# A linear-attention and MLP block: M built from whole 80-column windows inside tile 0's product, Q's weights permuted on chip, and six more short zero matmuls at the start

## The chip, the cores and the metric

The kernel runs on one core of one Trainium2 chip. The metric is the device time in microseconds of one execution. The kernel before took 210.43 us, the median of 9 runs (209.28 to 211.49).

## The reference

Everything is in bf16, with S = 2048 tokens, D = 640, 32 heads of 20 dimensions, and F = 1536. Cut to what matters:

```python
xn = layernorm(x)
# A: linear attention
q, k, v = split(xn @ wqkv)                     # 32 heads of 20
phi = lambda t: where(t > 0, t + 1, exp(t)) + 1e-6
pq, pk = phi(q), phi(k)
kv  = einsum("bhsd,bhse->bhde", pk, v)         # per head 20 x 20
z   = sum over s of pk
num = einsum("bhqd,bhde->bhqe", pq, kv)
den = einsum("bhqd,bhd->bhq", pq, z) + 1e-6
A = (num / den) @ wo
# B: MLP
B = gelu(xn @ w1 + b1) @ w2 + b2
out = x + A + B
```

## The kernel before

A small planner (`Planner.ins`) records every instruction by hand in the order of its engine's queue, works out which semaphores it has to wait for from the resources it reads and writes, and leaves out waits that the engine already knows of and TensorE's waits for itself. Each engine then runs its own list in order. Nothing is reordered later: the order in the source is the order on each queue.

The tokens are 16 tiles of 128, in 4 chunks of 512. D is 5 blocks of 128 and F is 12. The eight banks of PSUM are handed out in a ring (`take`).

1. **Start (L255 to L425).** SP loads x tile by tile and W1 in four pieces. `filler(9)` runs nine 512-column matmuls on zeros on TensorE. VectorE and GpSimd work out tile 0's norm, TensorE transposes tile 0 (`transp2`, L313), ScalarE and VectorE copy it to `xnT` (L321, L322), a tiny transpose (L303) turns b1, one more filler follows, and then the units of the MLP's first product begin (`h_unit`, L381: five matmuls and a gelu on ScalarE, L385). Tiles 1 and 2 are transposed by TensorE among the units ("T1" and "T2" in `plan`), all later tiles by DMA (`xnT_dma`, L245) after VectorE's norm (L354). Units of tiles 0 to 3 take one tile each, then two pairs of tiles, then two groups of four.
2. **K (L475 to L484).** 160 matmuls (L480) and `phi`: exp on ScalarE (L468), two steps on VectorE (L469, L471).
3. **G (L489 to L497).** G = xn^T phi(K), 160 matmuls (L492) into `GTb`, while VectorE sums phi(K) over the tiles into `zsum` in fp32 (L501, L504) and splits the sum into a high and a low bf16 part `zhl` (L506, L507).
4. **Q (L525 to L533).** For each chunk and each j of 5, five 512-column matmuls (L529) and `phi`. The 128 rows of block j are the columns j, j+5, j+10, ... of Q's weights, so each head has four rows in each block, and the weights are loaded with a step of 5. After chunk 0 come `z_step` (z per row, L512, and the masked `ZB`, L518) and `kvt_step` (L538): V's weights times G, masked by VectorE to the heads' blocks (L542), into the zeroed `KVT`.
5. **M and the denominator (L546 to L575).** M = blockdiag(kv) Wo in Q's row order (`m_step`): for each j and each half of the columns, two windows of rows by four groups of 32 columns of the array, 80 matmuls (L554), copied to `Msb` by ScalarE (L563) or VectorE (L560). Then `den_all`: 20 matmuls (L569), + 1e-6 (L573) and the reciprocal (L575).
6. **Spread and scale.** `spread` copies the reciprocals, 32 heads per chunk, by four DMAs of 32 KB per chunk to the 128 rows of Q's layout (`rsp`); chunk 0's are issued by ScalarE, the others by SP. `scale_pq` multiplies a chunk of phi(Q) by it in one VectorE step (L579). `x_again` (SP) loads x once more.
7. **Output (L612 to L662).** `out_mm` accumulates, for each tile, 12 products of the gelu with W2 and 5 of phi(Q) with M, in two halves of 320 columns (L618). The W2 part of tiles 0 to 3 is done first, then their phi(Q) part, then tiles 4 to 15 in one go; VectorE adds x + b2 (L594, L629) and SP stores. The last tile goes in pieces of 320, 192 and 128 columns.

Of the kernel before, what the change touches and what calls it, by code (L numbers as in the profile page):

```python
# [5 lines left out]
ALU = AluOpType  # L6
ACT = mybir.ActivationFunctionType
P = 128
# [104 lines left out]
def bass_parallel_sum__linear_attn_block__dense_activation_gelu__prompt_kernel(  # L113
# [13 lines left out]
    assert DH == 4 * DT and NC == 4 and P == 4 * H and DT * F >= 2 * (DT + 1) * D  # L127
# [4 lines left out]

    e0 = [DH * ((P * t) // DH) for t in range(DT)]
    e1 = [DH * (-((-(P * (t + 1))) // DH)) for t in range(DT)]
    Wd = [e1[t] - e0[t] for t in range(DT)]

    with contextlib.ExitStack() as es:
# [15 lines left out]
        KVT = W1f[:, DT * D:2 * DT * D].rearrange("p (k d) -> p k d", k=DT)  # L153
        Wqkv = sb("Wqkv", [P, DT, 3 * D], BF16)
        W2 = sb("W2", [P, JT, D], BF16)
        Wo = sb("Wo", [P, DT, D], BF16)
# [9 lines left out]
        hmask = sb("hmask", [P, H], BF16)  # L166
        maskKV = [sb(f"maskKV{t}", [P, Wd[t]], BF16) for t in range(DT)]
# [11 lines left out]
        rsp = sb("rsp", [P, NC, CW], BF16)  # L179
# [31 lines left out]
        r_Wq, r_Wv, r_W2, r_Wo = R_("Wq"), R_("Wv"), R_("W2"), R_("Wo")  # L211
# [12 lines left out]
        r_KVT = R_("KVT")  # L224
        r_M = [R_("M%d" % j) for j in range(DT)]
        r_zsum, r_zhl, r_z, r_ZB = R_("zsum"), R_("zhl"), R_("z"), R_("ZB")
        r_den, r_rden = R_("den"), R_("rden")
        r_rsp = [[R_("rsp%d_%d" % (c, r)) for r in range(4)] for c in range(NC)]
# [59 lines left out]
        for t in range(DT):  # L288
            band(maskKV[t][:], r_masks, P * t - e0[t], Wd[t] // DH, DH)
        band(hmask[:], r_hmask, 0, H, 4)  # L290
# [5 lines left out]
        def filler(n):  # L296
            b = take(1)
            Pl.ins(pe, [lambda e: e.matmul(bank(b), warm[:, 0:P], warm[:], start=True, stop=True)  # L298
                        for _ in range(n)], reads=[r_warm], writes=[B_[b]])
# [93 lines left out]
        filler(9)  # L393
        ln_half(0, 0)
# [60 lines left out]
        dma("sync", Wo[:], A_wo.rearrange("(k p) n -> p k n", p=P), [r_Wo])  # L455
# [31 lines left out]
        Pl.ins(g, lambda e: e.memset(KVT.bitcast(FP32), 0.0), writes=[r_KVT] + r_W1)  # L487
# [11 lines left out]
        def z_sums():  # L499
            a, c = tord[0], tord[1]  # L500
            Pl.ins(v, lambda e: e.tensor_tensor(out=zsum, in0=PK[:, a, :], in1=PK[:, c, :], op=ALU.add),  # L501
                   reads=[r_PK[a], r_PK[c]], writes=[r_zsum])
            for t in tord[2:]:
                Pl.ins(v, lambda e, t=t: e.tensor_tensor(out=zsum, in0=zsum, in1=PK[:, t, :], op=ALU.add),  # L504
                       reads=[r_PK[t], r_zsum], writes=[r_zsum])
            Pl.ins(v, lambda e: e.tensor_copy(zhl[:, 0, :], zsum), reads=[r_zsum], writes=[r_zhl])  # L506
            Pl.ins(v, lambda e: e.tensor_tensor(out=zhl[:, 1, :], in0=zsum, in1=zhl[:, 0, :], op=ALU.subtract),  # L507
                   reads=[r_zsum, r_zhl], writes=[r_zhl])

        def z_step():  # L510
            b = take(1)
            Pl.ins(pe, [(lambda e, j=j, i=i: e.matmul(bank(b, j, j + 1), zhl[:, i, j:D:DT], onesm[:, 0:1],  # L512
                                                      start=(i == 0), stop=(i == 1)))
                        for j in range(DT) for i in range(2)],
                   reads=[r_zhl, r_ones], writes=[B_[b]])
            Pl.ins(v, lambda e: e.tensor_copy(z_sb[:], bank(b, 0, DT)), reads=[B_[b]], writes=[r_z])
            for j in range(DT):
                Pl.ins(v, lambda e, j=j: e.tensor_scalar(ZB[:, j, :], hmask[:], z_sb[:, j:j + 1], None, ALU.mult),  # L518
                       reads=[r_z, r_hmask], writes=[r_ZB])
# [5 lines left out]
        def q_chunk(c):  # L525
            cc = slice(c * CW, (c + 1) * CW)
            for j in range(DT):
                b = take(1)
                Pl.ins(pe, [(lambda e, k=k, j=j, b=b: e.matmul(  # L529
                    bank(b), Wqkv[:, k, j:D:DT], xnT[:, k, cc],  # L530
                    start=(k == 0), stop=(k == DT - 1))) for k in range(DT)],
                    reads=[r_Wq] + sum(r_xnT[c * CH:(c + 1) * CH], []), writes=[B_[b]])
                phi(bank(b), b, 1, PQ[:, j, cc], r_PQ[c][j], [])  # L533

        def kvt_step():
            for t in range(DT):
                b = take(1)
                Pl.ins(pe, [(lambda e, k=k, b=b, t=t: e.matmul(  # L538
                    bank(b, 0, Wd[t]), Wqkv[:, k, 2 * D + t * P:2 * D + (t + 1) * P],
                    GTb[:, k, e0[t]:e1[t]], start=(k == 0), stop=(k == DT - 1))) for k in range(DT)],  # L540
                    reads=[r_Wv] + r_GT, writes=[B_[b]])
                Pl.ins(v, lambda e, b=b, t=t: e.tensor_tensor(  # L542
                    out=KVT[:, t, e0[t]:e1[t]], in0=bank(b, 0, Wd[t]), in1=maskKV[t][:], op=ALU.mult),
                    reads=[B_[b], r_masks], writes=[r_KVT])

        def m_step():  # L546
            for j in range(DT):
                b = (0, 2, 4, 0, 2)[j]
                fns = []
                for h in range(2):  # L550
                    for i in range(2):
                        for q in range(4):
                            c0 = j + 32 * DT * q
                            fns.append(lambda e, t=q + i, q=q, i=i, h=h, b=b, c0=c0: e.matmul(  # L554
                                bank(b + h, 0, HW)[32 * q:32 * q + 32, :],
                                KVT[:, t, c0:c0 + 31 * DT + 1:DT], Wo[:, t, h * HW:(h + 1) * HW],
                                start=(i == 0), stop=(i == 1)))
                Pl.ins(pe, fns, reads=[r_KVT, r_Wo], writes=B_[b:b + 2])
                if j in (2, 4):
                    Pl.ins(v, lambda e, b=b, j=j: e.tensor_copy(halves(Msb[:, j, :]), pair(b)),  # L560
                           reads=B_[b:b + 2], writes=[r_M[j], r_zsum, r_zhl])
                else:
                    Pl.ins(s_, lambda e, b=b, j=j: e.activation(halves(Msb[:, j, :]), pair(b), ACT.Copy),  # L563
                           reads=B_[b:b + 2], writes=[r_M[j], r_zsum, r_zhl])

        def den_all():
            b = 6
            for j in range(DT):
                Pl.ins(pe, [(lambda e, j=j, c=c: e.matmul(  # L569
                    bank(b)[H * c:H * c + H, :], ZB[:, j, :], PQ[:, j, c * CW:(c + 1) * CW],  # L570
                    start=(j == 0), stop=(j == DT - 1))) for c in range(NC)],
                    reads=[r_ZB] + [r_PQ[c][j] for c in range(NC)], writes=[B_[b]])
            Pl.ins(v, lambda e: e.tensor_single_scalar(den_sb[:], bank(b), 1e-6, ALU.add),  # L573
                   reads=[B_[b]], writes=[r_den])
            Pl.ins(v, lambda e: e.reciprocal(rden[:], den_sb[:]), reads=[r_den], writes=[r_rden])  # L575

        def scale_pq(c):
            cc = slice(c * CW, (c + 1) * CW)
            Pl.ins(v, lambda e: e.tensor_tensor(  # L579
                out=PQ[:, :, cc], in0=PQ[:, :, cc],  # L580
                in1=rsp[:, c:c + 1, :].broadcast_to((P, DT, CW)), op=ALU.mult),
                reads=r_rsp[c] + r_PQ[c], writes=r_PQ[c])

        def spread(c):
            for r in range(4):
                dma(s_ if c == 0 else "sync", rsp[r:P:4, c, :], rden[H * c:H * c + H, :], [r_rsp[c][r]],
                    reads=[r_rden])
# [14 lines left out]
        ring[0] = 3  # L602
# [3 lines left out]
        m_step()  # L606
        den_all()
        for c in range(NC):
            spread(c)
        scale_pq(0)  # L610

        def out_mm(t, lo, hi, b, w0, w1):  # L612
            tok = slice(t * P, (t + 1) * P)
            seq = [(HG[:, jb, tok], W2[:, jb, :], [r_HG[t][jb], r_W2]) for jb in range(JT)]
            seq += [(PQ[:, j, tok], Msb[:, j, :], [r_PQ[t // CH][j], r_M[j]]) for j in range(DT)]
            n = len(seq)
            for i in range(lo, hi):
                Pl.ins(pe, [(lambda e, i=i, x=x, bb=bb: e.matmul(  # L618
                    bank(bb, 0, x[1] - x[0]), seq[i][0], seq[i][1][:, x[0]:x[1]],
                    start=(i == 0), stop=(i == n - 1))) for x, bb in zip(w0, w1)],  # L620
                    reads=seq[i][2], writes=[B_[bb] for bb in w1], mark=(i in (JT - 1, n - 1)))
# [12 lines left out]
        ahead = [4, 0, 2, 6]  # L634
        for t, b in enumerate(ahead):
            out_mm(t, 0, JT, b, HALF, [b, b + 1])
# [6 lines left out]
        ring[0] = 4  # L643
# [7 lines left out]
        t = NT - 1  # L651
        xb(t)
# [49 lines left out]
```

## Time and profile before

| | |
|---|---|
| median of 9 runs | 210.43 us (209.28 to 211.49) |
| the nine runs | 209.28, 209.30, 209.71, 209.78, 210.43, 210.69, 210.98, 211.40, 211.49 |
| profiled execution, its own time | 210.98 us |
| its span, first to last instruction | 209.3 us |
| TensorE busy | 205.1 us (98%) |
| VectorE / ScalarE / GpSimd busy | 108.5 / 74.4 / 20.1 us |
| chain that ended last: TensorE | 96% of the span |

The profile is one execution. Times in it are microseconds from the span's start unless marked ns. An engine that is not the bottleneck loses nothing by being idle. Matmuls are pipelined, so the length of one in the profile is more than the distance to the next one; distances between starts, or counts in a window, tell the pace. Where a line of the profile names an idle time, it also names what ended it; "issue" is time in which the engine waited for nothing that the profile shows.

### The profile page before, as it was taken

Reading aid. Unit: us, or ns where it says so; the run is one execution under the profiler, and the core shown is the slowest. Engines: PE = TensorE matmul, PEld = TensorE weight load, DVE = VectorE, ACT = ScalarE, POOL = GpSimd, SP = SyncE. Lnnn points to the kernel's source line nnn. Section 1 sums busy time; section 2 is a strip of 40 time slices with the busy share of each in tenths; the row PEclk is TensorE's granted clock in tenths of the full one; section 3 lists DMA queues with packets and bytes.
Section 4 is the critical chain, followed back from the end, with each engine's and each line's share of the span. In section 5 each row is a group of like instructions: output and inputs, shape, how many; then the busy total and the mean of one; then the engine's idle time right before and its main releaser. Section 6 shows DMA issues by size and latency. Waiting matters only on the chain.

```text
span 209.3 us, 3967 instructions
## 1 busy us (share of the span) xinstructions
PE 205.1 (98%) x1622; PEld 142.5 (68%) x1622; DVE 108.5 (52%) x213; ACT 74.4 (36%) x146; POOL 20.1 (10%) x57
## 2 busy tenths in 40 slices
PE   7999999999999999999999999999999999999995
PEld 2799888444457777777757556677777777777775
DVE  4588864000005888999048898733753422523322
ACT  2499888666667544211153556100000000000000
POOL 2144436700011000000000000000000000000000
DMA  5975995899300000000000001952110110000002
GB/s 166 351 242 103 134 169 105 267 307 376 115 0 0 0 3 0 3 0 0 0 3 0 0 2 21 357 170 61 63 66 31 53 45 31 31 34 31 31 31 66
DMA packets 23371, 18.16 MB, mean 87 GB/s; under 512 B 9912, under 2 KB 23352, under 8 KB 23352
## 3 DMA queue, kind: packets, MB, share of 16 engines
q1 hardware_dynamic: 23136, 17.77, 29.4%
q8 instruction: 13, 0.21, 0.4%
q10 hardware_dynamic: 216, 0.13, 0.3%
q14 instruction: 6, 0.05, 0.1%
HBM read 12.62 MB, written 2.62 MB: 73 GB/s over the span
## 4 chain that ended last, share of the span: by engine, by line
PE 96%; DVE 1%; DMA 1%; issue 0%
PE ps L618 35%; PE ps L381 26%; PE ps L492 10%; PE ps L480 10%; PE ps L529 10%; PE ps L554 1%; DMA xPK<-in_A_x_dram 1%; DVE stats L326 1%; PE ps L538 1%; PE ps L313 1%; PE ps L569 1%; PE ps L298 0%; PE ps L512 0%; DVE W L659 0%; DVE xn_tm L354 0%
## 5 line engine op out<-in xcount | busy, mean ns | idle before, releaser
L618 PE MATMUL ps<-W,HG 128*128 128x320 bf16 (+2 forms) x396 | 54.6, 295 | 0.0
L381 PE MATMUL ps<-xnT,W 128*128 128x128 bf16 (+2 forms) x480 | 54.3, 277 | 0.1
L381 PEld LDWEIGHTS ps<-xnT,W 128*128 128x128 bf16 x480 | 38.2, 101 | 15.8 <-issue 0.5
L618 PEld LDWEIGHTS ps<-W,HG 128*128 128x128 bf16 x396 | 38.1, 98 | 14.6 <-issue 0.4
L385 ACT ACTIVATE HG<-ps,b1c 128x128 bf16<-128x128 f32 (+2 forms) x96 | 41.8, 474 | 13.4 <-PE ps L381 11.7
L629 DVE TENSOR_TENSOR W<-ps,xnT 128x640 bf16<-128x640 f32 x15 | 12.4, 824 | 36.9 <-PE ps L618 36.6
L468 ACT ACTIVATE ek<-ps 128x512 bf16<-128x512 f32 (+1 forms) x36 | 23.2, 645 | 20.7 <-PE ps L529 11.0
L469 DVE TENSOR_SCALAR ek<-ek 128x512 bf16<-128x512 bf16 (+1 forms) x36 | 10.9, 303 | 37.8 <-ACT ek L468 36.6
L618 PE MATMUL ps<-Msb,PQ 128*128 128x320 bf16 (+2 forms) x165 | 24.2, 295 | 0.0
L529 PE MATMUL ps<-xnT,Wqkv 128*128 128x512 bf16 x100 | 21.9, 379 | 0.0
L492 PE MATMUL ps<-xPK,xn_tm 128*128 128x320 bf16 x160 | 21.9, 299 | 0.0
L480 PE MATMUL ps<-Wqkv,xnT 128*128 128x320 bf16 x160 | 21.9, 299 | 0.0
L618 PEld LDWEIGHTS ps<-Msb,PQ 128*128 128x128 bf16 x165 | 15.9, 98 | 5.9
L480 PEld LDWEIGHTS ps<-Wqkv,xnT 128*128 128x128 bf16 x160 | 15.7, 98 | 6.2
L492 PEld LDWEIGHTS ps<-xPK,xn_tm 128*128 128x128 bf16 x160 | 15.7, 98 | 6.1
L529 PEld LDWEIGHTS ps<-xnT,Wqkv 128*128 128x128 bf16 x100 | 11.7, 118 | 9.5
L326 DVE BATCH_NORM_STATS2 stats<-xPK 128x6 f32<-128x320 bf16 x32 | 15.1, 472 | 4.2 <-DMA xPK<-in_A_x_dram 3.6
L471 DVE SCALAR_TENSOR_TENSOR PQ<-ps,ek 128x512 bf16<-128x512 f32 x20 | 13.8, 691 | 2.1
L471 DVE SCALAR_TENSOR_TENSOR xPK<-ps,ek 128x640 bf16<-128x640 f32 x16 | 13.2, 824 | 1.7
L504 DVE TENSOR_TENSOR Msb<-Msb,xPK 128x640 f32<-128x640 f32 x14 | 11.6, 826 | 0.5
L496 ACT ACTIVATE W<-ps 128x640 bf16<-128x640 f32 x5 | 3.5, 704 | 18.2 <-PE ps L492 18.2
L354 DVE TENSOR_SCALAR xn_tm<-xPK,aggr,rstd 128x640 bf16<-128x640 bf16 (+2 forms) x17 | 7.3, 433 | 2.5 <-POOL rstd L342 1.3
(57 smaller groups left out, 77.9 us busy)
## 6 DMA issues: line engine op xcount, KB each, us to landing
xnT<-in_A_x_dram SPq DMA_DIRECT2D x4, 640.0 KB, 6.1
Wqkv<-in_A_wqkv_dram SPq DMA_DIRECT2D x3, 800.0 KB, 6.5
out_dram<-W SPq DMA_DIRECT2D x15, 160.0 KB, 1.8
W<-in_B_w_dram SPq DMA_DIRECT2D x4, 480.0 KB, 6.0
W<-in_B_w_dram SPq DMA_DIRECT2D x1, 1920.0 KB, 16.0
xPK<-in_A_x_dram SPq DMA_DIRECT2D x2, 640.0 KB, 6.3
Wo<-in_A_wo_dram SPq DMA_DIRECT2D x1, 800.0 KB, 10.6
xPK<-in_A_x_dram SPq DMA_DIRECT2D x4, 160.0 KB, 3.9
```

The lines of the kernel that those rows point to most:

```text
L326: Pl.ins(v, lambda e: e.bn_stats(stats[:, s, 6 * h:6 * h + 6], x_in[:, t, h * HW:(h + 1) * HW]), reads=r_x[t], writes=[r_stats[s]])
L381: Pl.ins(pe, [(lambda e, k=k: e.matmul(bank(b, 0, w), W1[:, k, jb * P:(jb + 1) * P], xnT[:, k, tok], start=(k == 0), stop=(k == DT - 1))) ...
L385: Pl.ins(s_, lambda e: e.activation(HG[:, jb, tok], bank(b, 0, w), ACT.Gelu_apprx_tanh, bias=b1c[:, jb:jb + 1]), reads=[B_[b], r_b1c], wri ...
L468: Pl.ins(s_, lambda e: e.activation(e2, src, ACT.Exp), reads=br, writes=[r_ek[s]])
L469: Pl.ins(v, lambda e: e.tensor_scalar(et, et, 1.0, 1e-6, ALU.min, ALU.add), reads=[r_ek[s]], writes=[r_ek[s]])
L471: Pl.ins(v, lambda e: e.scalar_tensor_tensor(out=d2, in0=src, scalar=0.0, in1=e2, op0=ALU.max, op1=ALU.add), reads=br + [r_ek[s]], writes= ...
L480: fns.append(lambda e, k=k, h=h, b=b, t=t: e.matmul(bank(b + h, 0, HW), xnT[:, k, t * P:(t + 1) * P], Wqkv[:, k, D + h * HW:D + (h + 1) * ...
L492: Pl.ins(pe, [(lambda e, t=t, h=h, b=b, f=f, i=i: e.matmul(bank(b + h, 0, HW), xn_tm[:, t, f * P:(f + 1) * P], PK[:, t, h * HW:(h + 1) * H ...
L504: Pl.ins(v, lambda e, t=t: e.tensor_tensor(out=zsum, in0=zsum, in1=PK[:, t, :], op=ALU.add), reads=[r_PK[t], r_zsum], writes=[r_zsum])
L529: Pl.ins(pe, [(lambda e, k=k, j=j, b=b: e.matmul(bank(b), Wqkv[:, k, j:D:DT], xnT[:, k, cc], start=(k == 0), stop=(k == DT - 1))) for k in ...
L618: Pl.ins(pe, [(lambda e, i=i, x=x, bb=bb: e.matmul(bank(bb, 0, x[1] - x[0]), seq[i][0], seq[i][1][:, x[0]:x[1]], start=(i == 0), stop=(i = ...
L629: Pl.ins(v, lambda e: e.tensor_tensor(out=halves(out_sb[:, s, :]), in0=pair(b), in1=halves(x_res[:, t, :]), op=ALU.add), reads=B_[b:b + 2] ...
```

## The change

- At the start, `filler` takes a width, and six 128-column zero matmuls follow the nine of 512 columns.
- The row order of Q's blocks is new. Blocks 0 and 1 hold dimensions 0 to 7 and 8 to 15 of heads 0 to 15, blocks 2 and 3 those of heads 16 to 31, and block 4 dimensions 16 to 19 of all 32 heads. GpSimd copies Q's weights in this order, 25 copies of 128 columns, over K's weights, which are no longer needed by then. Q's matmuls load them without a step; they wait for all 25 copies (`r_WqP`). `zhl` is written in the same order, in ten smaller VectorE steps.
- KV is built in 8 windows of 4 heads (80 columns), each over the 128 rows from `E0[w]`: 40 matmuls into two banks and three masking steps on VectorE. Wo is loaded as 8 overlapping windows of the same rows by 8 DMAs. Four GpSimd copies make from it `KVP`: the 32 columns of each window and block, side by side; for block 4, two windows share 32 columns and the other 16 are zero.
- M then takes, for each half of the columns, four matmuls per block (one window for each group of 32 columns) and eight for block 4: 48 instead of 80, in groups that each signal on their own; each half is copied by itself, the first by ScalarE and the second by VectorE.
- The order after Q: half the columns of tile 0's W2 product, the denominator's matmuls, M in the order 0, 1, 4, 2, 3 (den + 1e-6 on VectorE after the copies of block 1), the reciprocal, all spreads, the scaling of chunk 0, the other half of tile 0's W2 product into the bank that held the denominator, and then tiles 1 to 3.
- The spread is three DMAs of 128 KB per chunk, whose source repeats each head's row for 8 or 4 rows; all twelve are issued by ScalarE. `rsp` lies in the memory of `xn_tm`. A chunk is scaled in three VectorE steps.

The diff, cut to its core:

```diff
-        def filler(n):
+        def filler(n, w=512):
             b = take(1)
-            Pl.ins(pe, [lambda e: e.matmul(bank(b), warm[:, 0:P], warm[:], start=True, stop=True)
+            Pl.ins(pe, [lambda e: e.matmul(bank(b, 0, w), warm[:, 0:P], warm[:, 0:w], start=True, stop=True)
                         for _ in range(n)], reads=[r_warm], writes=[B_[b]])
...
         filler(9)
+        filler(6, P)
...
-        dma("sync", Wo[:], A_wo.rearrange("(k p) n -> p k n", p=P), [r_Wo])
+        for w in range(NW):
+            dma("sync", Wo[:, w, :], A_wo[E0[w]:E0[w] + P, :], [r_Wo[w]])
...
+        Pl.ins(g, lambda e: e.memset(KVP[2], 0.0), writes=[r_KVP[2]] + r_W1)
+        for k in range(DT):
+            for i in range(DT):
+                Pl.ins(g, lambda e, k=k, i=i: e.tensor_copy(plain(Wqkv[:, k, D:2 * D], i), parts(Wqkv[:, k, 0:D], i)),
+                       reads=[r_Wq], writes=[r_Wk, r_WqP])
...
-                    bank(b), Wqkv[:, k, j:D:DT], xnT[:, k, cc],
+                    bank(b), Wqkv[:, k, D + j * P:D + (j + 1) * P], xnT[:, k, cc],
...
+            for i in range(2):
+                Pl.ins(g, lambda e, i=i: e.tensor_copy(
+                    KVP[i].rearrange("p w (h t) -> p w h t", t=TA), kt[:, :, :, TA * i:TA * i + TA]),
+                    reads=r_KVT, writes=[r_KVP[i]] + r_W1)
...
+        def m_step(js, bs, after):
+            for n, (j, b) in enumerate(zip(js, bs)):
+                for h in range(2):
+                    fns, reads = [], []
+                    for a in range(2 if j == DT - 1 else 1):
                         for q in range(4):
...
+                    Pl.ins(pe, fns, reads=reads, writes=[B_[b + h]])
+                    m_copy(j, b, h)
+                if n == 1:
+                    after()
...
+            for r, (h, n) in enumerate(((0, HH), (HH, HH), (0, H))):
+                src = rdv[H * c + h:H * c + h + n].broadcast_to((n, P // n, CW))
+                dma(s_, rsp[:, c, r, :], src, [r_rsp[c][r]] + (sum(r_xn, []) if c + r == 0 else []),
                     reads=[r_rden])
...
-        m_step()
-        den_all()
-        for c in range(NC):
-            spread(c)
-        scale_pq(0)
+        b0 = take(2)
+        ahead = [(b0 + 2 * i) % 8 for i in range(4)]
...
-        ahead = [4, 0, 2, 6]
-        for t, b in enumerate(ahead):
+        out_mm(0, 0, JT, b0, HALF[:1], [b0])
+        den_mm(b0 + 1)
+        m_step([0, 1, DT - 1, 2, 3], ahead[1:] + ahead[1:3], lambda: den_eps(b0 + 1))
+        den_rec()
+        for c in range(NC):
+            spread(c)
+        scale_pq(0)
+        out_mm(0, 0, JT, b0, HALF[1:], [b0 + 1])
+        for t in range(1, 4):
+            b = ahead[t]
             out_mm(t, 0, JT, b, HALF, [b, b + 1])
```

## The prediction

> **What bounds the kernel now.** I read the busy table first, then the chain of waits, then the pace of the matmuls in windows, and last the timelines of the three places that the change touches. The busy table and the chain say the same: TensorE is the bound from 5.8 us to the end.
>
> ```profile
> PE 205.1 (98%) x1622; PEld 142.5 (68%) x1622; DVE 108.5 (52%) x213; ACT 74.4 (36%) x146; POOL 20.1 (10%) x57
> ```
>
> ```profile
> 5.76 0.72 PE ps L313 x5
> 6.48 0.12 PE ps L303
> 6.60 0.54 PE ps L298
> 7.14 1.60 PE ps L381 x15
> 8.74 0.53 PE ps L313 x5
> ...
> 22.57 0.09 issue
> ...
> 105.29 5.39 PE ps L529 x25
> 110.68 0.36 PE ps L512 x10
> 111.05 1.58 PE ps L538 x25
> 112.63 16.19 PE ps L529 x75
> 128.82 3.03 PE ps L554 x80
> 131.85 1.08 PE ps L569 x20
> 132.93 74.06 PE ps L618 x561
> ```
>
> In the second fence, the chain, the columns are start, length, what. So only three things move the end: fewer or faster matmuls, a stall that goes, or a new stall. No step of VectorE, ScalarE or GpSimd shows after 5.8 us until the last eviction. The middle (M at L554, the denominator at L569, the product with V at L538) is 5.69 us of PE.
>
> The second reading is the pace. The windows of the line L381 alone count its matmuls (busy of PE with its count, then of the weight loads, then granted clock, DMA share, GB/s):
>
> ```profile
> 9.10:10.00 0.90, 0.90 (x9) 0.90 (x10) 1.00 1.08 349
> 10.20:11.10 0.90, 0.90 (x20) 0.90 (x18) 1.00 1.10 332
> ```
>
> The same 128-column matmul starts every 107 ns up to 10.05 us and every 56 ns from there on: the array runs at half speed for the first 8.8 us of its work. The clock column stays 1.00 and does not show it; the counts do. The nine 512-column fillers before, from 1.25, start every 427 ns, at half speed too. The timeline has the one real hole in that stretch:
>
> ```profile
> 4.21 1.06 PE L298 MATMUL ps<-warm 128*128 128x512 bf16 x2
> 5.76 0.72 PE L313 MATMUL ps<-ident,xn_tm 128*128 128x128 bf16 x5 [0.49 <-DVE xn_tm L354]
> ```
>
> The last filler starts at 4.64 and streams to 5.07, tile 0's transposes start at 5.76: 0.69 us empty. After 6.53 the stream is unbroken, and full speed comes 3.5 us later.
>
> **The change part by part, against the profiled execution** (span 209.3, its own time 210.98: 1.7 lies around the span; the median of the nine is 210.43, so this was one of the longer ones).
>
> *Six fillers in front of the transposes.* At 107 ns they take 0.64 us of the 0.69: the hole closes, and tile 0's transposes come at most 0.1 late. What it can bring is an earlier full speed. If an unbroken stretch of some 3.5 us is what brings it (6.53 to 10.05 here), then in the changed kernel the stretch runs from 1.25 and the switch comes before the real work at 6.95. The 30 matmuls that start between 6.95 and 10.05 then cost 56 instead of 107 ns: 30 x 0.051 = 1.53 us. Is it kept? PE next stops at 22.41, for 0.25 us ("issue" in the chain), until tile 5's transposed x, issued at 17.92 and landed at 22.57. That transpose hangs on VectorE's chain of norms, which itself waited for PE's transposes twice (1.8 and 0.7 us, at 9.31 and 13.40), so it moves forward too, by about 1.5. ScalarE keeps up: its evictions follow each other every 0.28 us, which is PE's 5 x 56 ns. I take -1.5, bounds -1.7 and 0. The nine times fit: 4 lie at 209.28 to 209.78 and 5 at 210.43 to 211.49, as if some executions had the early switch already; I expect all to have it, so both ways of counting (210.98 - 1.5, or the lower group's 209.5) give 209.5 after this part.
>
> [...]
>
> *Weights of Q permuted by GpSimd (25 copies of 128 columns), contiguous loads.* Q's 100 matmuls go at 216 ns for 512 columns whatever the load; the strided load (118 ns, against 98 for contiguous ones) is hidden in them: 0. The copies are new work. They can start when K's projection ends (83.6) and the first Q matmul (105.1) waits for all 25. GpSimd shows no copy; the nearest rows are a 128-column memset at 205 ns and selects at 293 to 421, each 70 ns apart since every copy waits for the one before: 25 x 0.275 = 6.9 to 25 x 0.49 = 12.3 us. I take the 293 ns row, the only one of 128 columns that also reads: 9.1 us, done at 93, hidden under G's 21.7. What is lost if the cover goes is rival two.
>
> *z in parts.* VectorE's two steps (0.49 and 0.82) become ten of 128 columns, some 0.2 to 0.3 each from the small rows (0.23 for ZB), 2.5 instead of 1.3 us, due at 110.5, done before at 99.7: 0.
>
> *KV product.* 25 matmuls of 140 to 160 columns become 40 of 80. Bounds per matmul: 40 ns (z's ten one-column matmuls, 0.36 us with a load each) and 60 (140 columns). At 80 columns streaming alone is 34, so I take the load's 40: 1.60 for 1.58, +0.02, at worst +0.8. VectorE's five masks (1.5 us) become three (some 0.49, 0.41 and 0.25, estimated from the evictions of 320, 192 and 128 columns at 492, 357 and 292 ns): a little less. Four GpSimd copies follow, at most 2 us, with 16 us of Q as cover: 0.
>
> *M.* Today 80 matmuls run as 20 groups of four side by side, 136 ns a group, 2.7 us, and two waits for evictions make it 3.03. After: 12 groups, 1.63. -1.40. The twelve evictions are halves: ScalarE 0.44, VectorE 0.49 (its 320-column row); banks come back before their second use by some 0.05 us, so up to 0.2 could be lost.
>
> *Order.* Half of tile 0's W2 product (12 x 136 ns = 1.63) now stands ahead of the denominator and covers the last phi: VectorE ends it 1.8 us after Q's last matmul, PE needs it after 1.63 + 0.86. A new wait stands behind M: the second half writes the bank of the denominator and waits until den + eps is read. VectorE has two evictions of M ahead of that: 0.47 until the first is ready, 2 x 0.45, then 0.68, and PE is told at 2.05 after M's start, while M ends at 1.65: +0.35 (0 to 0.6). Queued behind it on PE is everything, so it counts fully.
>
> *Reciprocal, spread, scale.* Reciprocal (3.35) starts after three more evictions: it ends 9.8 us after Q's end, 8.9 today. The spread is 3 x 128 KB per chunk instead of 4 x 32, all twelve on ScalarE's queue, 0.77 us an issue, 2.3 us to landing, 3.0 for the bigger ones: chunk 0 is complete at 14.4, its last scale step at 14.9 after Q's end. PE comes to it at 1.63 + 1.08 + 1.63 + 0.35 + 1.63 + 9.78 = 16.1; slack 1.2, today 2.1. 0. SP loses the spread, and its stores stand no later. Wo in eight DMAs moves W2 on SP by 8 x 0.43 - 0.43 = 3.0 us; W2 lands at 55.7 today and is needed at 129: 0.
>
> Sum: -1.50 + 0.02 - 1.40 + 0.35 = -2.53; 210.98 - 2.53 = **208.5**.
>
> **The rivals.** *One: the front brings nothing*, because the switch is no earlier (the transposes or the one-row bias transpose at 6.41 still break the stretch), or because tile 5's transpose, which took 4.65 us to land where others took 2.6, lands no earlier and PE only waits longer at 22.4. Then the middle's -1.03 alone is left: 209.9 from the profiled run, 209.4 from the median. For it: nothing in the trace tells how full a stretch must be.
>
> *Two, the slower one: GpSimd's copies come late.* One row shows GpSimd held up by VectorE, and one the sums that lie over the copies' cover:
>
> ```profile
> 34.82 0.45 DVE L354 TENSOR_SCALAR xn_tm<-xPK,aggr,rstd 128x640 bf16<-128x640 bf16 x1 [1.07 <-POOL rstd L342]
> 34.95 0.53 POOL L280 TENSOR_SCALAR_AFFINE_SELECT maskKV<-maskKV 128x140 bf16<-128x140 bf16 x1
> 35.55 0.34 POOL L284 TENSOR_SCALAR_AFFINE_SELECT maskKV<-maskKV 128x140 bf16<-128x140 bf16 x1
> ```
>
> ```profile
> 86.35 12.01 DVE L504 TENSOR_TENSOR Msb<-Msb,xPK 128x640 f32<-128x640 f32 x14
> ```
>
> The select that began under a VectorE step took 0.53, the same select alone 0.34. The 14 of the last row and one before them run back to back from 85.5 to 98.4. If they take turns, about 4 copies are done by 85.5, then 15 turns of 0.86 + 0.30 end at 103, six more among z's small steps at 106: PE waits 0 to 1.5 us. If GpSimd is shut out until the sums and z's parts end at 101, 21 copies of 0.28 to 0.49 end at 107 to 111: PE waits 1.8 to 6, and the time is 210.3 to 214.5. From a wait of 3.0 us on, so copies of over 0.35 us shut out, it is slower than before by more than 0.5%.
>
> [...]
>
> *Three: the middle waits longer*, den + eps by 0.6 more, or the spread's bigger packets land over 1.2 us late and PE stalls at tile 0's PQ part: 209.5 to 212.
>
> **How the numbers follow.** Forecast 0.44 (207.8 to 209.3, all faster). Rival one 0.20, half faster, half within 0.5%, which is about what a measurement here can tell from no change (1.05 us). Rival two 0.25: 0.12 within, 0.13 slower. Rival three 0.11: 0.05 within, 0.06 slower. Faster 0.54, same 0.27, slower 0.19. The range goes from 207.7 to 211.6: above it lie the worst of rivals two and three (0.15), below it a few in a hundred.
>
> **What would show it.** Right: L381's windows count 20 matmuls per 0.9 us from about 7 us; units of tile 4 start near 21.2 instead of 22.66; the first Q matmul follows G without a gap; M's 48 matmuls take 1.6 to 1.8; one gap of 0.3 to 0.4 before the second half of tile 0. Wrong: the half-speed pace lasts to 10 us; PE waits for GpSimd at Q; single copies of 0.8 us and more among VectorE's sums; PE waits for a scale step.

## The result, and the profile after

The changed kernel took 208.16 us, the median of 21 runs (207.85 to 208.63). The kernel before, run beside it and over all its runs, took 209.53 us, the median of 63 (208.97 to 211.49). The ratio is 0.9923, with a 95% interval of 0.9906 to 0.9941: faster by 0.6 to 0.9%. The medians are 1.37 us apart, the means (208.18 and 209.79) 1.61. The two profiled executions took 210.98 and 208.41 us, 2.57 apart: the one of before was among its longer ones, so what the profiles show between them is more than what the medians show.

First the busy table, then the chain that ended last (start, length, what), both of the changed kernel. Line numbers are those of the changed kernel: L322 are tile 0's and 1's transposes, L390 the MLP's first product, L557 Q, L540 z, L567 the product with V, L674 the output product, L621 the denominator, L611 M, L596 M's evictions on VectorE, L627 den + 1e-6.

```profile
PE 202.0 (98%) x1611; PEld 137.8 (67%) x1611; DVE 111.6 (54%) x230; ACT 73.8 (36%) x148; POOL 33.9 (16%) x83
```

```profile
5.76 0.54 PE ps L322 x5
...
6.78 1.00 PE ps L390 x15
...
21.10 0.20 issue
...
103.93 5.40 PE ps L557 x25
109.32 0.23 PE ps L540 x10
109.55 1.46 PE ps L567 x40
111.01 16.19 PE ps L557 x75
127.20 1.63 PE ps L674 x12
128.83 1.19 PE ps L621 x20
130.02 0.30 PE ps L611 x8
130.32 0.02 issue
130.34 0.89 DVE Msb L596 x2
131.23 0.61 DVE den_sb L627
131.84 0.05 issue
131.89 72.49 PE ps L674 x549
```

Three readings. The first 15 matmuls of L390 take 1.00 us instead of 1.60: in this execution they start every 56 ns from the first one on, in that of before every 107 ns. G (up to 103.93) runs into Q without a gap, although VectorE and GpSimd now both work beside it. And from Q's end to the second half of tile 0 there are 131.89 - 127.20 = 4.69 us with half of tile 0's product (1.63) inside, so 3.06 for the denominator, M and a wait, where the kernel before needed 132.93 - 128.82 = 4.11. These pieces are bounded partly by a matmul's end and partly by a start, so I also count between starts alone: from Q's last matmul to the last matmul of all it is 77.33 us, before 78.31, so 0.98 less. At the end of that stretch the chain leaves TensorE: two evictions of M and den + 1e-6 on VectorE are what the second half waits for. The chain's piece of M is short only because the chain went over to VectorE there; its 48 matmuls start from 129.84 to 131.35.

The weight copies on GpSimd, from the page, and the sums beside them, from the timeline:

```profile
L510 POOL COPY Wqkv<-Wqkv 128x128 bf16<-128x128 bf16 x25 | 15.1, 603 | 22.9 <-PE ps L491 21.4
```

```profile
84.99 12.00 DVE L528 TENSOR_TENSOR Msb<-Msb,xPK 128x640 f32<-128x640 f32 x14
```

The mean of 603 ns hides two sizes: about 294 ns before VectorE's sums and after them, 797 ns beside them, one copy to a sum at a distance of 0.86 us. The last copy ends at 98.93, 4.7 us before Q's first weight load (103.63). The 14 sums take 12.00 us, as they did without the copies (12.01).

### The profile page after: what moved, and what is told of

It reads as the page before. It is cut to its first block, busy times and chain, and to the rows that moved or that the text cites. A ratio compares the mean times of both kernels' runs of the same rounds, so it can differ in the third digit from the quotient of the medians.

```text
span 206.7 us, 4001 instructions
## 1 busy us (share of the span) xinstructions
PE 202.0 (98%) x1611; PEld 137.8 (67%) x1611; DVE 111.6 (54%) x230; ACT 73.8 (36%) x148; POOL 33.9 (16%) x83
## 3 DMA queue, kind: packets, MB, share of 16 engines
q10 hardware_dynamic: 1752, 1.58, 4.1%
## 4 chain that ended last, share of the span: by engine, by line
PE 95%; DVE 2%; DMA 1%; issue 0%
PE ps L674 36%; PE ps L390 26%; PE ps L516 11%; PE ps L491 11%; PE ps L557 10%; DMA xPK<-in_A_x_dram 1%; DVE stats L335 1%; PE ps L567 1%; PE ps L621 1%; DVE Msb L596 0%; PE ps L322 0%; DVE den_sb L627 0%; PE ps L307 0%; PE ps L611 0%; DVE W L723 0%
## 5 line engine op out<-in xcount | busy, mean ns | idle before, releaser
L674 PE MATMUL ps<-W,HG 128*128 128x320 bf16 (+2 forms) x396 | 54.8, 295 | 0.2 <-DVE den_sb L627 0.2
L390 PE MATMUL ps<-xnT,W 128*128 128x128 bf16 (+2 forms) x480 | 53.1, 272 | 0.3 <-issue 0.2
L674 PEld LDWEIGHTS ps<-W,HG 128*128 128x128 bf16 x396 | 38.1, 98 | 14.8 <-DVE den_sb L627 0.5
L390 PEld LDWEIGHTS ps<-xnT,W 128*128 128x128 bf16 x480 | 36.8, 98 | 16.2 <-issue 0.7
L674 PE MATMUL ps<-Msb,PQ 128*128 128x320 bf16 (+2 forms) x165 | 24.2, 295 | 0.0
L557 PE MATMUL ps<-xnT,Wqkv 128*128 128x512 bf16 x100 | 21.9, 379 | 0.0
L674 PEld LDWEIGHTS ps<-Msb,PQ 128*128 128x128 bf16 x165 | 15.9, 98 | 5.9
L510 POOL COPY Wqkv<-Wqkv 128x128 bf16<-128x128 bf16 x25 | 15.1, 603 | 22.9 <-PE ps L491 21.4
L557 PEld LDWEIGHTS ps<-xnT,Wqkv 128*128 128x128 bf16 x100 | 9.7, 98 | 11.4
L482 DVE SCALAR_TENSOR_TENSOR PQ<-ps,ek 128x512 bf16<-128x512 f32 x20 | 13.8, 691 | 2.1
L482 DVE SCALAR_TENSOR_TENSOR xPK<-ps,ek 128x640 bf16<-128x640 f32 x16 | 13.2, 823 | 1.7
```

The costliest lines, as they stand in the source:

```text
L390: Pl.ins(pe, [(lambda e, k=k: e.matmul(bank(b, 0, w), W1[:, k, jb * P:(jb + 1) * P], xnT[:, k, tok], start=(k == 0), stop=(k == DT - 1))) ...
L482: Pl.ins(v, lambda e: e.scalar_tensor_tensor(out=d2, in0=src, scalar=0.0, in1=e2, op0=ALU.max, op1=ALU.add), reads=br + [r_ek[s]], writes= ...
L510: Pl.ins(g, lambda e, k=k, i=i: e.tensor_copy(plain(Wqkv[:, k, D:2 * D], i), parts(Wqkv[:, k, 0:D], i)), reads=[r_Wq], writes=[r_Wk, r_WqP])
L557: Pl.ins(pe, [(lambda e, k=k, j=j, b=b: e.matmul(bank(b), Wqkv[:, k, D + j * P:D + (j + 1) * P], xnT[:, k, cc], start=(k == 0), stop=(k == ...
L674: Pl.ins(pe, [(lambda e, i=i, x=x, bb=bb: e.matmul(bank(bb, 0, x[1] - x[0]), seq[i][0], seq[i][1][:, x[0]:x[1]], start=(i == 0), stop=(i = ...
```

## The experiments

They are in the order of the questions: the start, the middle, GpSimd, and a version that fills what waits were found.

**The start: the six fillers taken out of the changed kernel.**

```diff
         filler(9)
-        filler(6, P)
```

> The changed kernel without the six short fillers. Theory (the fillers only take away the late switch to full speed, which about a quarter of the executions of the kernel before have): most executions at 207.9 to 208.6 like the changed kernel, but a quarter or so at 209 to 210.2; median within 0.3 us of 208.2. Rival (the fillers bring full speed earlier in every execution): nearly all executions 1 us or more later, median 209.2 or above. Second rival (the fillers do nothing at all): the narrow spread of the changed kernel, no execution above 208.9.

Measured: 208.48 us, the median of 12, in two heaps: seven at 207.87 to 208.65, five at 209.86 to 210.48. With the six fillers none of 21 was over 208.63. The profile fell on a late one (210.36). The windows of TensorE (busy with the count of matmuls, granted clock, DMA share, GB/s), this kernel first, the changed kernel second:

```profile
8.30:9.20 0.90, 0.90 (x12) 1.00 1.10 360
10.70:11.60 0.90, 0.90 (x20) 1.00 1.09 337
```

```profile
8.30:9.20 0.90, 0.90 (x20) 1.00 1.10 374
10.70:11.60 0.90, 0.90 (x20) 1.00 1.09 330
```

The late execution still runs at 107 ns a matmul at 9 us; its pace changes at 10.6. So in the changed kernel the fillers take away a late switch that about two in five of these executions had; they do not speed up the others. The theory stood, with more late ones than the quarter that it said.

**The start: the six fillers alone in the kernel before.**

```diff
         filler(9)
+        filler(6, P)
```

> The kernel before with the six fillers alone. Theory: no execution above 210.1, all at 209.0 to 209.9, median 209.3. Rival (earlier in every execution): median 208.0 to 208.5. Second rival (nothing): a quarter of the executions stay at 210 to 211.5.

Measured: 209.71 us, the median of 12 (209.13 to 210.37), ratio 1.0004 (0.9978 to 1.003). Of the 28 runs of before in the same comparison five were at 211.07 to 211.19; none is here, but two lie at 210.27 and 210.37, where the theory had none, and the mean does not differ (209.73 and 209.71). The median is 0.4 above the 209.3 that was expected. With five late runs in 28, none in 12 can be chance, so for the kernel before this run does not show that the fillers help. In the trace the six fillers run at 107 ns, from 5.07 to 5.71, the hole in front of the transposes shrinks to 0.13 us, and the pace changes inside the next filler, between 6.6 and 7.08, where the profiled execution of before, with its hole of 0.69, changed at 10.05:

```profile
5.80:6.90 1.10, 1.10 (x9) 1.00 1.11 357
7.30:8.20 0.90, 0.90 (x21) 1.00 1.07 346
```

**The start: a bigger hole in the kernel before.**

```diff
-        filler(9)
+        filler(4)
```

> The kernel before with four long fillers instead of nine, so that TensorE has nothing from about 3 us to 5.8. [...] Rival (the switch counts matmuls or hangs on luck, not on the hole): a mix of early and late, as before, median about 209.5.

Measured: 211.19 us, the median of 6 (210.29 to 211.63), ratio 1.0076 (1.0046 to 1.0105): all six are above 210.2 us, so by their times all are late, and the mix of early and late that the rival had did not come. The pace changes at 9.75 in the profile:

```profile
8.30:9.20 0.90, 0.90 (x11) 1.00 1.10 349
10.70:11.60 0.90, 0.90 (x20) 1.00 1.10 336
```

So in these runs the more solid the stretch before the real work, the rarer a late switch: six of six here, ten of 63 with the nine long fillers (five of 12 in the changed kernel), none of 21 in the changed kernel with the six short ones as well. The price of a late switch is 1 to 2 us: 2.08 between the medians of the two heaps of the changed kernel without the six (208.05 and 210.13), 1.36 between the starts of tile 4's units in the profiles of before and after (22.66 and 21.30). The hole alone does not decide: in the profile of the new order with the old M (below), which has no short fillers, TensorE is empty from 5.07 to 5.77, and the pace is 56 ns from 5.84 on. How solid the stretch has to be, and over how long, was not settled. Executions some 1 us above the lower heap are not explained; two of 12 in the run before and two of ten in the next one lie there, although both have the six fillers.

In the seven profiles of kernels with the six fillers the pace changes between 4.2 and 7.1 us; twice it is before 4.75, where a stretch of 3.5 us from the first filler on, as the prediction supposed it, would have ended. Why one and the same kernel has early and late executions no run shows.

**The middle: the old order with the new M.**

```diff
-        out_mm(0, 0, JT, b0, HALF[:1], [b0])
-        den_mm(b0 + 1)
-        m_step([0, 1, DT - 1, 2, 3], ahead[1:] + ahead[1:3], lambda: den_eps(b0 + 1))
+        m_step([0, 1, DT - 1, 2, 3], ahead[1:] + ahead[1:3], lambda: None)
+        den_mm(b0 + 1)
+        den_eps(b0 + 1)
+        out_mm(0, 0, JT, b0, HALF[:1], [b0])
```

> The changed kernel with the old order: M directly behind Q, then the denominator, den + 1e-6, and all of tile 0 after that. Theory (the new order hides the wait for the last phi on VectorE, behind which M's evictions stand): M's second use of its banks waits for evictions that stand behind two phi steps, 0.5 to 1.2 us of new gaps; the gap behind M goes (0.3), sum 0.2 to 0.9 us more, 208.4 to 209.1. Rival (only the fewer matmuls count, the order is worth nothing): 208.0 to 208.2.

Measured: 209.45 us, the median of 10 (209.23 to 210.40), ratio to before 0.9991 (0.9964 to 1.0018). The direction held, the size was a little larger than expected: 1.29 above the changed kernel. What TensorE waited for, in this run (us in total, times, longest):

```profile
PE ps L611 <- DVE PQ L482: 1.1, 2, 0.8
```

The end of its chain, in which the first 16 matmuls of M are missing because the chain went over to VectorE:

```profile
128.81 1.27 PE ps L611 x32
130.08 1.08 PE ps L621 x20
131.16 74.06 PE ps L674 x561
```

Two groups of M start 0.60 and 1.07 us after the group before them, where 0.14 is the rule. They are not where the theory had them: they are the fourth and the fifth of the 12, M's first use of their banks, and the second use comes without a wait. The two banks are those of Q's last two blocks. Each group starts 0.15 us after the phi step (L482) that reads its bank has ended (127.58 and 128.66, starts at 127.73 and 128.81). So what half of tile 0's product hides in the changed kernel is that the last two phi steps still read banks that M is to write. The kernel before keeps M off these two banks. The new M in the old order on other banks was not run, so how much of the 1.29 belongs to the order and how much to the banks stays open.

**The middle: the new order with the old M.** In the kernel before:

```diff
-        ring[0] = 3
+        ring[0] = 1
...
-        ahead = [4, 0, 2, 6]
-        for t, b in enumerate(ahead):
+        ahead = [6, 0, 2, 4]
+        out_mm(0, 0, JT, 6, HALF[:1], [6])
+        den_all()
+        m_step()
+        den_rec()
+        for c in range(NC):
+            spread(c)
+        scale_pq(0)
+        out_mm(0, 0, JT, 6, HALF[1:], [7])
+        for t in range(1, 4):
+            b = ahead[t]
             out_mm(t, 0, JT, b, HALF, [b, b + 1])
```

> The kernel before with the new order alone: half of tile 0's W2 product behind Q, then the denominator, the old M of 80 matmuls, the other half. Theory (the new M and the new order need each other: with the old order the new M loses its 1.1 us to waits for evictions behind VectorE's phi; the old M is bound by its own 20 groups of 136 ns, 2.7 us, so the order can only take its 0.3 us of waits): 0.0 to 0.4 below before, 209.1 to 209.5. Rival (the order is what brings the middle's gain, whatever M): 1.0 or more below, 208.5. Rival (the larger evictions of the old M stand in the way and PE waits for banks): 0.3 or more above before.

Measured: 209.42 us, the median of 12 (208.93 to 210.28), ratio 1.0002 (0.9986 to 1.0018): nothing. From its chain:

```profile
127.52 1.63 PE ps L615 x12
129.15 1.19 PE ps L569 x20
130.34 2.90 PE ps L554 x80
133.24 72.43 PE ps L615 x549
```

Without the half product, 4.09 us for the denominator and M (L554). From the start of Q's last matmul to that of the last matmul of all, the four combinations take: old M and old order 78.31 us, old M and new order 78.29, new M and old order 78.45, both new 77.33. On the banks of these runs neither part is worth anything alone: without the order the time of the 32 matmuls that were saved turns into waits for the last two phi steps, and without the smaller M there is hardly a wait for the order to hide (the old M has one distance of 0.28 us between groups in the old order and one of 0.27 in the new).

**The middle: the wait behind M.**

```diff
-        out_mm(0, 0, JT, b0, HALF[:1], [b0])
+        out_mm(0, 0, 8, b0, HALF[:1], [b0])
         den_mm(b0 + 1)
...
+        out_mm(0, 8, JT, b0, HALF[:1], [b0])
         out_mm(0, 0, JT, b0, HALF[1:], [b0 + 1])
```

> The changed kernel with 8 of the first half's 12 products of tile 0 ahead of the denominator and the other 4 behind M, ahead of the second half. Theory (the gap of 0.41 us behind M is the wait for den + 1e-6, and four products of 0.54 us cover it): the gap goes, the denominator starts 0.54 earlier and its last group just finds its phi, so 0.25 to 0.4 us less, 207.8 to 207.9. Rival (the gap is TensorE's change from 32-column groups to the whole array): no difference, 208.2. Second rival (the last phi comes too late for the earlier denominator): a new wait of 0.2 to 0.4 in front of its last group and no gain.

Measured: 208.25 us, the median of 9 (207.96 to 208.94), ratio to before 0.9938 (0.9911 to 0.9965), from the changed kernel not to be told apart. The profile does show what the theory said:

```profile
127.01 1.09 PE ps L674 x8
128.09 1.19 PE ps L621 x20
129.29 1.67 PE ps L611 x48
130.96 72.97 PE ps L674 x553
```

The next matmul starts 0.09 us after M has streamed, where it was 0.40 in the changed kernel. So 0.31 of the gap was the wait for den + 1e-6; the 0.09 that stay, as between tile 0's product and the denominator in the changed kernel, fit the rival, which put the gap down to the change of column groups; no run has that change apart. From Q's end (127.01) to the last matmul's end (203.93) there are 76.92 us, where the changed kernel has 204.38 - 127.20 = 77.18: 0.26 less. That this reaches the median is not shown by this run.

**GpSimd: the sums left out.** 13 of VectorE's 15 sums of phi(K) are left out, so that z is that of three tiles.

```diff
-            for t in tord[2:]:
+            for t in tord[2:3]:
```

> The changed kernel with 2 of VectorE's 15 sums of phi(K) over the tiles; the other 13 are left out. Theory (a GpSimd copy that reads and a VectorE sum with two inputs take turns, so each copy of about 0.29 us lasts as long as the sum beside it): nearly all 25 copies take 0.29 us at a distance of 0.36, the last ends near 91.5 instead of 98.9, and the time stays. Rival (the copies are slow by themselves in that stretch, whatever VectorE does): 0.80 us each and the end at 98.9 as before.

```profile
82.34 9.68 POOL L510 COPY Wqkv<-Wqkv 128x128 bf16<-128x128 bf16 x24 [21.44 <-PE ps L491]
```

Two copies, those beside the sums that are left, take 0.80 and 0.88 us, all others 0.30 at a distance of 0.36; the last ends at 92.4. The one run took 208.5. So a copy beside one of these sums is held up (0.80 us against 0.30), and the sums lose nothing: they follow each other every 0.86 us with the copies (changed kernel) and without them (before). It is not always the copy that waits: four smaller steps with two inputs, of 128 columns (L534), take 0.32 us beside the copies of this run, which keep their 0.30, and 0.29 with no copy beside them in the changed kernel. What holds up the one or the other was not shown.

**GpSimd: 55 copies.**

```diff
-        for k in range(DT):
+        for k in [0, 1, 2, 3, 4, 0, 1, 2, 3, 4, 0]:
             for i in range(DT):
                 Pl.ins(g, lambda e, k=k, i=i: e.tensor_copy(plain(Wqkv[:, k, D:2 * D], i), parts(Wqkv[:, k, 0:D], i)),
```

> The changed kernel with 55 instead of 25 weight copies on GpSimd, 30 of them the same again. Theory (copies are free until the last one ends past 103.9, where Q's first matmul is due; 0.36 us each once the sums are over): the last ends near 109.6, TensorE waits some 5.7 us before Q, 213.9. Rival (the copies have hidden costs elsewhere, on VectorE or TensorE): more than 7 us. Rival (the cover is larger than read): less than 4 us.

Measured: 216.41 us (216.31 and 216.51), ratio 1.0305 (1.0236 to 1.0374): 8 us more, where the wait alone was to be 5.7. The last copy ends at 109.96, near the 109.6 that was worked out. The line of Q's first matmuls says a wait of 6.18:

```profile
110.42 1.91 PE L557 MATMUL ps<-xnT,Wqkv 128*128 128x512 bf16 x4 [6.18 <-POOL Wqkv L510]
```

```profile
108.00:109.00 1.00, 0.00 (x0) 0.50 0.00 0
112.00:113.00 1.00, 1.00 (x4) 0.50 0.00 0
114.00:115.00 1.00, 1.00 (x6) 1.00 0.00 0
```

But the record of the very first matmul is missing from the trace (24 of the chunk's 25 are there), while its weight load is there, at 110.02. So TensorE waited 5.8 us, from G's end near 104.2 to 110.0, as the theory said (5.7). The rest is mostly its clock. In the second fence the granted clock is the figure behind the count of matmuls. It falls to half about 2.3 us after G's last matmul (the window from 106 to 107 has 0.77) and is back between 113 and 114. Until then eight matmuls start 427 ns apart instead of 216, which is 8 x 0.21 = 1.7 us. With G ending 0.3 us later than in the changed kernel's profile, 5.8 + 1.7 + 0.3 = 7.8, and the two profiled executions are 7.9 apart (216.31 and 208.41). The rival of hidden costs was right in its sum, with a cost that neither had named.

**A version that fills both waits**: the split half of above, and

```diff
-        for t, n in ((4, 2), (6, 2), (8, 4), (12, 4)):
+        plan += h_list(4, 1, 0, 2) + h_list(5, 1, 0, 2) + h_list(4, 2, 2, JT)
+        for t, n in ((6, 2), (8, 4), (12, 4)):
             plan += h_list(t, n, 0, JT)
```

> The changed kernel with tile 0's first half split 8 and 4, and with the first two units of tiles 4 and 5 done tile by tile, so that TensorE has 0.56 us of work on tile 4 while tile 5's transpose lands. Theory (both gaps, 0.3 behind M and 0.2 at 21.1, are waits that other work can fill): 0.45 to 0.6 less, 207.6 to 207.7. Rival (TensorE only waits a little later): 207.9 to 208.2.

Measured: 207.79 us, the median of 6 (207.67 to 207.98), ratio to before 0.9895 (0.9854 to 0.9935), 0.37 under the changed kernel, a little less than expected and in another comparison than the changed kernel's. TensorE's stream no longer stops at 21.1, nor behind M:

```profile
11.90 22.34 PE ps L390 x295
...
129.16 1.67 PE ps L612 x48
130.83 72.97 PE ps L675 x553
```

## Why the prediction was right, and where not

**The time.** 208.5 was forecast and 208.16 measured, but the parts of the sum have other shares than it gave them, and that the sum came out is in part luck. It started from a late execution (210.98) and took 1.50 off for the front, which led to where the median of before had been all along (209.53). From there the median moved by 1.37. In the traces 1.25 of this lies between the starts of Q's first matmul and of the last matmul of all (101.63 us before, 100.38 after); the other 0.12 is not assigned.

**The front (-1.50).** That a late switch costs 1 to 2 us and that a more solid stretch makes it rarer was right, and so was tile 5's transpose, which moved forward with VectorE's chain (landed at 21.21 after 22.57; PE there at 21.30 with a wait of 0.20 left, for a forecast of 21.2). Between the two profiled executions the front brought 22.66 - 21.30 = 1.36. The step that failed is the reading of the nine times. Five in nine seemed late; of 63 runs ten lie above 210.9 and 47 below 210. The median of before was an early execution all the time, so to the median the fillers bring about nothing (the run with the six alone: 1.0004). What they bring to the mean is not settled: nothing in the kernel before (209.73 and 209.71), 0.8 in the changed kernel (208.18 against 209.00 without them, in another comparison). What the profiled execution of the changed kernel shows is not the fillers' work either: its pace changed at about 4.3, before the first of the six. They then ran at 56 ns and ended at 5.02, and TensorE was empty until 5.76. So the hole was not closed, as forecast, but stayed at 0.74 us, and the full speed was there all the same.

**KV and z (+0.02).** Mis-sized: -0.25. The 40 matmuls of 80 columns go at 36 ns, not 40, so 1.46 us instead of 1.58; the load's 40 did not bound them. z's ten went from 40 ns, in the steady part, to 25 with the loads no longer stepped by 5 (0.36 to 0.23 us in all). The 40 that I took from z's row was the pace of stepped loads, and the contiguous ones went faster.

**M, the order and the wait (-1.40 + 0.35).** -1.05 forecast, -0.98 measured between starts (3.06 - 4.11 = -1.05 by the pieces of the chains). M's 12 groups at 136 ns and the wait behind M came as worked out (second half at 2.05 us after M's start; 129.84 to 131.89 measured). The prediction's own figures for that wait, 2.05 - 1.65, make 0.40, which is what it was; its sum has 0.35. That M and the order, on these banks, are only worth something together was not in the prediction; the two runs show it.

**The rivals.** One, with the middle's gain alone, describes the median, with 1.25 us in place of 1.03; its times (209.4 and 209.9) were too long because it too started from the nine runs, in which late ones are too many. Two had the right engine waiting and the wrong size. It reckoned 0.86 + 0.30 a turn. In the trace a copy starts 0.18 us after a sum, ends 0.15 us after that sum's end, while the next sum is already under way, and the next copy, which starts 0.06 us later, ends 0.15 us after that one; so a turn is 0.86, and the copies end at 98.93 instead of 103 to 106. The forecast's 0.29 for a copy alone was right, its "hidden at 93" not. Three did not come: den + 1e-6 was read in time and chunk 0's last scale step ended at 141.7, 1.6 us before PE came to it (1.2 forecast), though the bigger packets took 3.4 us to land, not 3.0.

## What to carry to other kernels

A kernel whose profile falls on one of two heaps of times is to be reckoned against the heap's share among many runs, not against the profiled one: a fix for the rare heap can narrow the spread and leave the median nearly where it was. Where fewer matmuls are bought, look at what still reads the banks that they write: here the saved matmuls were worth about 1 us with the product of another tile moved ahead of them, and nothing without it on the same banks. Work put on GpSimd should be reckoned at the pace that it has beside VectorE's steps: here a copy of 128 columns started every 0.86 us beside VectorE's sums, one to a sum, and every 0.36 us without them. That left 4.7 us of cover, and a wait of 5.8 us past the cover cost 1.7 us of TensorE's clock as well.

## What the runs showed of the hardware that was not expected

- A GpSimd copy of 128 columns takes 0.29 us alone and 0.80 beside a sum of 640 fp32 columns, while the sums keep their distance of 0.86 us (changed kernel and before).
- At the start of the profile of before the granted clock reads 1.00 while the same matmul goes at 107 ns, and at 56 from 10.05 us on; after a wait of 5.8 us, in the run with 55 copies, it reads 0.50 and the pace (427 ns for 512 columns, 216 at a clock of 1.00) agrees with it. So at the start the pace was read from the counts.
- After G the clock fell about 2.3 us after the last matmul and came back some 3.3 us after work began again, in the run with 55 copies.
- z's one-column matmuls, each with a weight load, start every 40 ns where the load has a step of 5 columns (before) and every 25 ns where it is contiguous (changed kernel).
